# Spreading the reloads of the half-transformed rows over the slots of a fused Fourier mixer and feed-forward kernel on Trainium2

## The chip, the cores and the metric

The kernel runs on one core of one Trainium2 chip. The time is device microseconds of one execution. The engines named below are TensorE (PE; PEld is its weight load), VectorE (DVE), ScalarE (ACT), GpSimd (POOL) and SyncE (SP). SP and POOL issue the DMAs, each in the order of its own queue.

## The reference

```
X  = rfft(x, axis=1)                       # x: 8 x 3008 x 256, float32
Yr = Xr @ w_r - Xi @ w_i + b_r             # Yi likewise, 256 x 256 weights
Y  = softshrink(Yr, 0.01) + 1j * softshrink(Yi, 0.01)
a  = irfft(Y, n=3008, axis=1)              # 8 x 3008 x 256 = 24064 tokens
h  = relu(a @ w_in)                        # 256 -> 2048
out = (s * h * h + b) @ w_out              # 2048 -> 256, float32
```

## The kernel before, in words

All transforms are matmuls with tables of cosines and sines. The Fourier transform over 3008 points is split in two steps: batches 0 and 1 use 94 x 32, batches 2 to 7 use 64 x 47, whose tables are other ones. A batch passes through these stages, each a list of units that one call returns:

- `s1_units(b)` (L677): the first step of the transform, one matmul of 512 columns a unit (L702; L700 for batch 1). Its result `u` is evicted to SBUF (L248 on ACT or L252 on DVE, whichever the planner's running load favours) and stored to the DRAM tensor `ud` (L706). Batches 2 to 7 have 12 units and 6 stores of 256 KB. After the last unit four loads `us <- ud` (L712, 384 KB each) bring the rows back in another order of partitions: this is the exchange that the two-step transform needs. The pool of `us` has four buffers.
- `fwd_units(b)` (L719): the second step from `us` (L729) into `xt`. For batch 1 it is part of the mix (L763).
- `mix_units(b)` (L741): 12 mix units a batch. Sums (L793), the mixing by the weights (L806), bias and soft threshold on DVE (L811 to L818) into `ring`, then an exchange of rows between the halves of the partitions. For the first ten units this row swap is four DMAs of 32 KB on SP (`ring <- ring`, L826), for the last two four copies on DVE (L828). The inverse step reads the swapped rows two steps of the list later (L836), and its result `v` is stored to `vd` (L845). After the last unit two loads `vs <- vd` (L852, 768 KB each) exchange again.
- `s4_units(b)` (L876): the last inverse step from `vs` (L892) into `yt`.
- the feed-forward layer over 48 tiles of tokens: `first_mm` (L947) with Relu on ACT (L954), the square on DVE or ACT (L961, L958), `second_mms` (L1005), the scaling (L1015) and the stores of `out` on SP (L973, L980, L988).

One tile of the feed-forward layer takes 16 slots. A slot holds two matmuls of L947 and four of L1005, and a written plan says which units of the other stages go into which slot: `schedule(start, span, units)` spreads a list evenly over `span` slots. `mark[b]` is the slot at which batch b's tiles begin: 0, 96, 192, 272, 368, 464, 560, 656. So while the tiles of batch b-2 run, batch b goes through its first step and batch b-1 through its mix.

The plan gives the order in which the work is recorded. The tile framework then sets the order on each engine and the waits: POOL and SP start a DMA when their queue reaches it and its waits are met, not at a slot. Every DMA on SP takes the next of eight completion semaphores, and waits for the DMA eight places before it on SP to land.

The two tables of the second kind of transform, `F_v` (576 KB, into the buffer of `F_t`, L386) and the one in `T_t` (768 KB, L388), are loaded by POOL once batch 1 no longer reads the old ones: by `load_tables_2` (L384).

Of the kernel before, what the change touches and what calls it, by code (L numbers as in the profile page):

```python
# [9 lines left out]
F16 = mybir.dt.float16  # L10
# [4 lines left out]
P = 128  # L15
# [9 lines left out]
SLOTS = 48  # L25
GROUPS = 32
# [139 lines left out]
def kernel(  # L166
# [13 lines left out]
    nc = tc.nc  # L180
    B, S, D = x.shape
# [47 lines left out]
    uspool = ctx.enter_context(tc.tile_pool(name="usp", bufs=4))  # L229
# [13 lines left out]
    def evac(dst, src, cols, scale=None):  # L243
        ta, td = 0.17 + cols / 1200.0, 0.15 + cols / 960.0
        if load["act"] + ta <= load["dve"] + td:
            load["act"] += ta
            if scale is None:
                return None, nc.scalar.copy(out=dst, in_=src)  # L248
            return None, nc.scalar.mul(out=dst, in_=src, mul=scale)
        load["dve"] += td  # L250
        if scale is None:
            return nc.vector.tensor_copy(out=dst, in_=src), None  # L252
        return nc.vector.tensor_scalar_mul(out=dst, in0=src, scalar1=scale), None
# [8 lines left out]
    def any_bank():  # L262

        turn_of[0] += 1
        if "h" in pools:
            return (other_bank, one_bank)[turn_of[0] % 2]()
        return (mix_bank, one_bank, mix_bank, other_bank)[turn_of[0] % 4]()
# [4 lines left out]
    def one_bank():  # L272
        return fpool.tile([P, 512], F32, name="psf", tag="psf")
# [110 lines left out]
    def load_tables_2(i):  # L384
        if i == 0:
            nc.gpsimd.dma_start(out=F_v, in_=F_v_d)  # L386
        else:
            nc.gpsimd.dma_start(out=T_t, in_=T_v_d)  # L388
# [69 lines left out]
    us = {}  # L458
# [7 lines left out]
    def first_batch():  # L466
# [138 lines left out]
        def last_dft(ec, n):  # L605
# [17 lines left out]
            )  # L623

        more = s1_units(1, True)

        def some(n):
# [45 lines left out]


    UCH = XCH // 2

    def s1_units(b, more_banks=False):  # L677

        old = b == 1
        rows, n = (96, N2) if old else (P, XH)  # L680
        ud = dpool.tile([rows, n, D], F16, name="ud", tag="ud")
        hold = {}
        if old:
            xts[b] = bigpool.tile([P, 2 * DC * CLASSES * L1], F16, name="xt", tag="xt")

        def unit(i):
            c, j = divmod(2 * i, XCH)
            k, ju = divmod(2 * i, UCH)
            if ju == 0:
                if old and k % 2:  # L690
                    w = UCH * D
                    hold["u"] = xts[b][:, k // 2 * w : k // 2 * w + w].rearrange(
                        "p (j d) -> p j d", d=D
                    )
                else:
                    hold["u"] = upool.tile([P, UCH, D], F16, name="u", tag="u")
            ps = any_bank() if more_banks else one_bank()
            rhs = x16[(b, c)][:, j * D : (j + 2) * D]
            if old:
                nc.tensor.matmul(ps[0:96, :], A_t[0:N1, :], rhs[0:N1], start=True, stop=True)  # L700
            else:
                nc.tensor.matmul(ps, A_2, rhs, start=True, stop=True)  # L702
            u = hold["u"]
            evac(u[0:rows, ju : ju + 2, :], ps[0:rows].rearrange("p (j d) -> p j d", j=2), 512)
            if ju == UCH - 2:
                nc.sync.dma_start(out=ud[:, k * UCH : (k + 1) * UCH, :], in_=u[0:rows])  # L706
            if i == n // 2 - 1:
                p, g = (P, 6) if old else (2 * SLOTS, GROUPS // 4)
                uv = ud.rearrange("k n d -> (k n) d").rearrange("(q p) d -> p q d", p=p)
                for q in range(4):  # L710
                    t = uspool.tile([P, g, D], F16, name="us", tag="us")
                    nc.sync.dma_start(out=t[0:p], in_=uv[:, g * q : g * q + g, :])  # L712
                    us[(b, q)] = t

        return [lambda i=i: unit(i) for i in range(n // 2)]

    xts = {}

    def fwd_units(b):  # L719

        cuts = [(lo, 5) for lo in range(0, 20, 5)] + [(lo, 4) for lo in range(20, GROUPS, 4)]

        def unit(lo, w, dc):
            if b not in xts:
                xts[b] = bigpool.tile([P, 2, DC, CLASSES * L1], F16, name="xt", tag="xt")
            ps = one_bank()
            for j in range(w):
                q, g = divmod(lo + j, GROUPS // 4)
                nc.tensor.matmul(  # L729
                    ps[:, j * 96 : (j + 1) * 96],  # L730
                    us[(b, q)][0:96, g, dc * P : (dc + 1) * P], F_v[:, lo + j, :],
                    start=True, stop=True,
                )
            evac(
                xts[b][:, :, dc].rearrange("p r (x j) -> p r x j", j=GROUPS)[..., lo : lo + w],
                ps[:, 0 : w * 96].rearrange("p (j r x) -> p r x j", r=2, x=SLOTS), w * 96,
            )

        return [lambda c=c, dc=dc: unit(*c, dc) for c in cuts for dc in range(DC)]
# [136 lines left out]
    def s4_units(b):  # L876

        groups = []
        for lo in range(0, N2, 5):
            for ec in range(DC):  # L880
                groups.append((lo, min(5, N2 - lo), ec))

        def unit(g):
            n2, w, ec = groups[g]
            if g == 0:
                shape = [P, DC, N2, 96] if b == 1 else [P, DC, SLOTS * L1]
                yts[b] = ypool.tile(shape, F16, name="yt", tag="yt")
            yt = yts[b]
            ps = one_bank()
            for j in range(w):  # L890
                h, k = divmod(n2 + j, HW)
                nc.tensor.matmul(  # L892
                    ps[:, j * 96 : (j + 1) * 96],
                    vs[(b, h)][:, k, ec * P : (ec + 1) * P], C_t if b == 1 else C_2,
                    start=True, stop=True,
                )
            if b == 1:
                evac(
                    yt[:, ec, n2 : n2 + w, :],
                    ps[:, 0 : w * 96].rearrange("p (j n) -> p j n", n=96), w * 96,  # L900
                )
                return
            evac(
                yt[:, ec].rearrange("p (n h m) -> p h n m", h=2, m=N2)[..., n2 : n2 + w],
                ps[:, 0 : w * 96].rearrange("p (m h n) -> p h n m", h=2, n=SLOTS), w * 96,
            )
            if g == len(groups) - 1:
                pr, half = divmod(b, 2)
                if half == 0:
                    tails[pr] = tpool.tile([P, DC, 2, TAIL], F16, name="tail", tag="tail")  # L910
                nc.gpsimd.tensor_copy(out=tails[pr][:, :, half], in_=yt[:, :, N - TAIL : N])

        return [lambda g=g: unit(g) for g in range(len(groups))]
# [112 lines left out]
    plan = {}  # L1026

    def schedule(start, span, units):
        for i, u in enumerate(units):
            plan.setdefault(start + (i * span) // len(units), []).append(u)  # L1030
# [19 lines left out]
    plan.setdefault(18, []).append(load_x_2)  # L1050
    schedule(24, 42, mix_units(1))
    for i in range(2):
        plan.setdefault(66 + 6 * i, []).append(lambda i=i: load_tables_2(i))
    schedule(mark[1] - 11, 16, s4_units(1))
    for b in range(2, B):
        s0, s1, s2 = mark[b - 2], mark[b - 1], mark[b]
        if b == 2:
            schedule(s0 + 36, 22, s1_units(b))
            schedule(s1 - 16, 18, fwd_units(b))
        else:  # L1060
            schedule(s0 + 2, s1 - s0 - 48, s1_units(b))
            schedule(s1 - 28, 14, fwd_units(b))
        schedule(s1 + 3, s2 - s1 - 31, mix_units(b))
        schedule(s2 - 14, 12, s4_units(b))
        if b + 1 < B:
            plan.setdefault(s1 - 26, []).append(lambda b=b: emit_load_x(b + 1))
# [43 lines left out]
```

## Time and profile before

| | us |
|---|---|
| three runs | 852.38, 855.0, 859.67 (median 855.0) |
| the profiled execution, its time | 853.03 |
| the profiled execution, its span | 851.2 |
| PE busy in the span | 834.9 (98%) |
| DVE, ACT, POOL busy in the span | 691.8 (81%), 645.8 (76%), 53.9 (6%) |
| mean of bytes moved | 115 GB/s |
| us <- ud, L712 | 28 DMAs of 384 KB |
| ring <- ring, L826 | 280 DMAs of 32 KB |

The profile is of one execution. A row of the waits gives the waiting engine and line, what it waited for, the time in all, how often, and the longest. A row of the timeline gives start, duration, engine, line and operation, output and input; x4 says that four such instructions were merged, and what stands in brackets is the idle time before it and what ended it. SPq rows are the issuing of DMAs, not their moving. The windows give, for a stretch of the span, the busy time of PE, PEld, DVE, ACT and POOL, then the granted clock of PE (1.00 is full speed), the DMA share and GB/s.

### The profile page before, as it was taken

The page shows a single profiled execution, that of the slowest core. Times are in us where ns is not written, and L with a number is a line of the kernel's source. Part 1 is how long each engine was busy: PE and PEld are TensorE (multiplying, and loading weights), DVE is VectorE, ACT ScalarE, POOL GpSimd, SP SyncE. Part 2 cuts the span into 40 slices and gives each one's busy share as a digit, 9 for nine tenths or more (in the row PEclk, how much of TensorE's full clock was granted, in tenths as well). Part 3 has the DMA queues.
Part 4 walks back from the last instruction along what each step waited for, and adds up shares of the span by engine and source line. Part 5 has one row for each costly group of instructions (what it writes and reads, how often), then busy time and mean ns, then how long its engine had stood idle before and what let it go on. Part 6 is the DMA issues. An engine that isn't in the chain of part 4 may idle for free.

```text
span 851.2 us, 17222 instructions
## 1 busy us (share of the span) xinstructions
PE 834.9 (98%) x6726; PEld 599.1 (70%) x6726; DVE 691.8 (81%) x999; ACT 645.8 (76%) x849; POOL 53.9 (6%) x87
## 2 busy tenths in 40 slices
PE   8999999999999989999999999999999999999998
PEld 7857766777777657667776677766677776766766
DVE  5999976888889868888888887888888888776675
ACT  5988867778777867787787878788776877766663
POOL 4540100000000000000000000000000000000000
PEclk9999999999999999999999999999999999999999
DMA  8965785156723673145731548123650222401111
GB/s 198 186 165 136 187 199 162 44 129 156 179 74 84 157 198 107 57 118 135 199 89 52 134 141 197 36 75 118 159 137 29 58 89 90 112 32 38 38 44 51
DMA packets 110505, 97.70 MB, mean 115 GB/s; under 512 B 11212, under 2 KB 99280, under 8 KB 109080
## 3 DMA queue, kind: packets, MB, share of 16 engines
q1 hardware_dynamic: 103480, 80.61, 33.4%
q0 software_dynamic: 6944, 16.00, 11.3%
q8 instruction: 53, 0.87, 0.4%
q14 instruction: 28, 0.23, 0.1%
HBM read 55.34 MB, written 46.66 MB: 120 GB/s over the span
## 4 chain that ended last, share of the span: by engine, by line
PE 88%; DMA 3%; ACT 3%; DVE 3%; issue 2%; POOL 0%; SPq 0%; DVEq 0%; ACTq 0%; POOLq 0%
PE psa L1005 36%; PE psh L947 36%; PE psf L806 4%; PE psf L892 2%; PE psf L836 2%; PE psf L793 2%; PE psf L729 2%; PE psf L702 2%; ACT rt L954 1%; DMA x<-in_x_dram 1%; DMA ring<-ring 1%; PE psm L528 1%; DMA vd<-v 1%; DMA vs<-vd 1%; DVE gt L961 1%
## 5 line engine op out<-in xcount | busy, mean ns | idle before, releaser
L954 ACT ACTIVATE rt<-psh 128x1024 f32<-128x1024 f32 (+2 forms) x384 | 386.9, 1008 | 129.0 <-PE psh L947 128.3
L961 DVE TENSOR_TENSOR gt<-rt 128x1024 f16<-128x1024 f32 (+2 forms) x315 | 377.3, 1200 | 104.3 <-ACT rt L954 102.7
L1005 PE MATMUL psa<-w_out_t,gt 128*128 128x256 f16 (+1 forms) x3024 | 455.6, 273 | 0.1
L1005 PEld LDWEIGHTS <-gt 128*128 128x128 f16 (+1 forms) x3024 | 302.2, 101 | 187.0 <-issue 2.3
L947 PE MATMUL psh<-yt,w_in 128*128 128x512 f16 (+1 forms) x1344 | 398.9, 380 | 0.2 <-ACT rt L954 0.2
L947 PEld LDWEIGHTS <-w_in 128*128 128x128 f16 x1536 | 141.5, 98 | 25.2 <-issue 1.9
L1015 DVE SCALAR_TENSOR_TENSOR ost<-psa,s_bc,bias_bc 128x512 f32<-128x512 f32 (+2 forms) x97 | 71.0, 732 | 15.7 <-PE psa L1005 14.9
L958 ACT ACTIVATE gt<-rt 128x1024 f16<-128x1024 f32 (+2 forms) x69 | 72.6, 1053 | 1.5
L248 ACT CAST v<-psf 128x512 f16<-128x512 f32 x79 | 45.8, 580 | 23.4 <-PE psf L836 23.4
L811 DVE TENSOR_TENSOR ring<-psf,s 128x512 f16<-128x512 f32 x84 | 57.5, 685 | 2.5 <-PE psf L806 1.0
L947 PE MATMUL psh<-tail,w_in 128*128 128x512 f16 (+1 forms) x192 | 52.2, 353 | 0.0
L806 PE MATMUL psf<-W_g,xt 128*128 128x256 f16 x336 | 50.4, 273 | 0.1
L248 ACT CAST xt<-psf 128x480 f16<-128x480 f32 (+3 forms) x74 | 43.0, 581 | 9.3 <-PE psf L729 8.2
L248 ACT CAST yt<-psf 128x480 f16<-128x480 f32 (+2 forms) x68 | 41.0, 622 | 11.4 <-PE psf L892 10.8
L248 ACT CAST u<-psf 128x512 f16<-128x512 f32 (+1 forms) x68 | 40.0, 588 | 1.0 <-PE psf L702 0.9
L816 DVE TENSOR_TENSOR ring<-ring,low 128x512 f16<-128x512 f16 x84 | 35.6, 423 | 2.3
L836 PE MATMUL psf<-ring,T_t 128*128 128x256 f16 x168 | 33.0, 275 | 4.3 <-DMA ring<-ring 4.1
L818 DVE TENSOR_TENSOR ring<-ring 128x512 f16<-128x512 f16 x84 | 35.5, 423 | 2.1
L817 DVE TENSOR_TENSOR ring<-ring,high 128x512 f16<-128x512 f16 x84 | 35.5, 422 | 2.0
L806 PEld LDWEIGHTS <-xt 128*128 128x128 f16 x336 | 32.9, 98 | 4.1 <-issue 0.2
L302 POOL DMA_DIRECT2D x<-in_x_dram x36 | 18.7, 528 | 237.4 <-PE psf L702 237.4
L892 PEld LDWEIGHTS <-vs 96*128 96x128 f16 x448 | 28.8, 97 | 6.7 <-issue 2.4
(114 smaller groups left out, 516.6 us busy)
## 6 DMA issues: line engine op xcount, KB each, us to landing
out_dram<-ost SPq DMA_DIRECT2D x170, 128.0 KB
us<-ud SPq DMA_DIRECT2D x28, 384.0 KB
vd<-v SPq DMA_DIRECT2D x42, 256.0 KB
vs<-vd SPq DMA_DIRECT2D x14, 768.0 KB
x<-in_x_dram POOLq DMA_DIRECT2D x36, 256.0 KB, 5.3
ud<-u SPq DMA_DIRECT2D x36, 256.0 KB
ring<-ring SPq DMA_DIRECT2D x280, 32.0 KB
out_dram<-ost SPq DMA_DIRECT2D x16, 120.0 KB
```

The lines of the kernel that those rows point to most:

```text
L248: return None, nc.scalar.copy(out=dst, in_=src)
L806: nc.tensor.matmul(ps[:, r, :], x_of(i, 1 - r)[:, dc], W_g[:, dc, r], start=(dc == 0), stop=(dc == DC - 1),)
L811: nc.vector.tensor_tensor(out=t, in0=ps, in1=hold[i // 2][:, i % 2].unsqueeze(1).to_broadcast([P, 2, D]), op=ALU.add,)
L816: nc.vector.tensor_tensor(out=m, in0=t, in1=low, op=ALU.max)
L836: nc.tensor.matmul(ps[:, j, :], T_t[:, 2 * i + j, :], z[:, j, :], start=True, stop=True)
L892: nc.tensor.matmul(ps[:, j * 96 : (j + 1) * 96], vs[(b, h)][:, k, ec * P : (ec + 1) * P], C_t if b == 1 else C_2, start=True, stop=True,)
L947: nc.tensor.matmul(o, w_in_t[dc][:, mc * P : (mc + 1) * P], r, start=(dc == 0), stop=(dc == DC - 1),)
L954: nc.scalar.activation(out=rt[:, :, 0:w], in_=ps[:, :, 0:w], func=AF.Relu)
L958: nc.scalar.activation(out=gt[:, :, 0:w], in_=rt[:, :, 0:w], func=AF.Square)
L961: nc.vector.tensor_tensor(out=gt[:, :, 0:w], in0=rt[:, :, 0:w], in1=rt[:, :, 0:w], op=ALU.mult)
L1005: nc.tensor.matmul(ps[0:size, h, :], gts[(ti, mc // 2)][:, mc % 2, sub * size : (sub + 1) * size], w_out_t[:, mc, :], start=(mc == 0), sto ...
L1015: nc.vector.scalar_tensor_tensor(out=ost[0:size, 0:k], in0=ps[0:size, 0:k], scalar=s_bc[0:size], in1=bias_bc[0:size].unsqueeze(1).to_broad ...
```

## The change

The four loads of `us` of batches 2 to 7 leave the last unit of the first step and become units of their own in the plan: for batch 2 at slots 69, 71, 73 and 75, for batches 3 to 7 at slots s1-48, -44, -40 and -36 (s1 is `mark[b-1]`). The first step of batches 3 to 7 is compressed by four slots, the forward units of batch 2 begin three slots later and end one later, and the two table loads are recorded at slots 54 and 80 instead of 66 and 72. Batch 1 keeps its four loads at the last unit. Some lines of the file move by one to seven.

```
@@ s1_units @@
-            if i == n // 2 - 1:
-                p, g = (P, 6) if old else (2 * SLOTS, GROUPS // 4)
-                uv = ud.rearrange("k n d -> (k n) d").rearrange("(q p) d -> p q d", p=p)
+            if i == n // 2 - 1 and old:
                 for q in range(4):
-                    t = uspool.tile([P, g, D], F16, name="us", tag="us")
-                    nc.sync.dma_start(out=t[0:p], in_=uv[:, g * q : g * q + g, :])
-                    us[(b, q)] = t
+                    load_us(q)
+
+        def load_us(q):
+            p, g = (P, 6) if old else (2 * SLOTS, GROUPS // 4)
+            uv = ud.rearrange("k n d -> (k n) d").rearrange("(q p) d -> p q d", p=p)
+            t = uspool.tile([P, g, D], F16, name="us", tag="us")
+            nc.sync.dma_start(out=t[0:p], in_=uv[:, g * q : g * q + g, :])
+            us[(b, q)] = t
+
+        us_loads[b] = [lambda q=q: load_us(q) for q in range(4)]
@@ the plan @@
     for i in range(2):
-        plan.setdefault(66 + 6 * i, []).append(lambda i=i: load_tables_2(i))
+        plan.setdefault(54 + 26 * i, []).append(lambda i=i: load_tables_2(i))
...
             schedule(s0 + 36, 22, s1_units(b))
-            schedule(s1 - 16, 18, fwd_units(b))
+            schedule(s0 + 69, 8, us_loads[b])
+            schedule(s1 - 13, 16, fwd_units(b))
         else:
-            schedule(s0 + 2, s1 - s0 - 48, s1_units(b))
+            schedule(s0 + 2, s1 - s0 - 52, s1_units(b))
+            schedule(s1 - 48, 16, us_loads[b])
             schedule(s1 - 28, 14, fwd_units(b))
```

In the built program the queue of POOL holds the same instructions in the same order, and both table loads wait for the same matmuls as before: F_v for the last L763 of batch 1, T_t for the last L836 of batch 1. The first instructions that stand elsewhere are, on PE, the forward units of batch 2, and on SP what follows the first `us` load of batch 2. The SP queue around the two places that matter below:

```
batch 2, before: last ud, us us us us, vd vd, out out, vd, vs vs
batch 2, after:  last ud, us, vd, us us, vd, out out, vd, us, vs vs
batch 4, before: swap 7, ud, last ud, swap 8, us us us us, out out, swap 9, vd
batch 4, after:  swap 7, last ud, us us, swap 8, out out, swap 9, vd, us us
```

For batches 3, 5, 6 and 7 the loads stand behind the last row swap both before and after. (The swaps named here are those of the preceding batch, whose mix runs beside the first step: for batch 4, of batch 3.)

More of the change, by code (lines that the diff above doesn't have):

```diff
@@ L675 @@
     UCH = XCH // 2
+    us_loads = {}
     def s1_units(b, more_banks=False):
```

## The prediction

> **What bounds the kernel now.** I read the page's busy times first, then who PE waits for, then the granted clock round those waits, then SP's queue just before them.
>
> ```profile
> PE 834.9 (98%) x6726; PEld 599.1 (70%) x6726; DVE 691.8 (81%) x999; ACT 645.8 (76%) x849; POOL 53.9 (6%) x87
> ```
>
> PE is busy for all but 16 us of the span. Some 8 of these lie in the start (4.7 us idle in the first 45 us) and the end (3.4 us in the last 51). The change adds or removes no matmul, so all that it can win is PE's waiting in between. The waits of PE from 60 us on:
>
> ```profile
> PE psf L836 <- DMA ring<-ring: 4.1, 3, 2.4
> PE psf L892 <- DMA vs<-vd: 1.8, 1, 1.8
> PE psf L892 <- ACT yt L248: 0.8, 3, 0.3
> PE psf L892 <- DVE yt L252: 0.6, 2, 0.3
> ```
>
> The reader should see that DMA makes PE wait at four moments only, 5.9 us in all. In PE's timeline they stand at 112.25 (0.44) and 114.57 (1.17), call them place A, at 139.02 (place B) and at 311.74 (place C):
>
> ```profile
> 139.02 0.39 PE L892 MATMUL psf<-C_t,vs 96*128 96x96 f16 x5 [1.82 <-DMA vs<-vd]
> ...
> 307.17 0.38 PE L836 MATMUL psf<-ring,T_t 128*128 128x256 f16 x2
> ...
> 311.74 0.62 PE L836 MATMUL psf<-ring,T_t 128*128 128x256 f16 x2 [2.44 <-DMA ring<-ring]
> ```
>
> A wait can cost more than its idle time. The windows just behind the three places (the column after the busy times is the granted clock):
>
> ```profile
> 115.10:118.70 3.60, 3.60 (x15) 2.32 (x14) 1.82 (x2) 2.19 (x3) 0.00 (x0) 0.53 0.38 126
> 139.10:143.00 3.90, 3.90 (x48) 3.03 (x49) 2.28 (x3) 3.10 (x6) 0.00 (x0) 1.00 0.50 144
> 313.30:316.70 3.40, 3.40 (x15) 1.82 (x13) 1.87 (x2) 1.66 (x3) 0.00 (x0) 0.51 0.63 197
> ```
>
> Behind A the clock is 0.53 for 3.6 us, which loses 3.6 x 0.47 = 1.7 us; behind C it is 0.51 for 3.4 us, again 1.7; behind B it stays 1.00. So A costs 1.6 + 1.7 = 3.3 us, B 1.8, C 2.4 + 1.7 = 4.1: together 9.2 us, 1.1% of the time. That is the ceiling.
>
> Why C waits is in SP's queue:
>
> ```profile
> 293.03 2.45 SPq L826 DMA_DIRECT2D ring<-ring  x4
> 295.58 1.01 SPq L706 DMA_DIRECT2D ud<-u  x2
> 296.69 3.06 SPq L826 DMA_DIRECT2D ring<-ring  x4
> 300.76 2.50 SPq L712 DMA_DIRECT2D us<-ud  x4
> 303.37 2.15 SPq L980 DMA_DIRECT2D out_dram<-ost  x2
> 305.62 3.49 SPq L826 DMA_DIRECT2D ring<-ring  x4
> ```
>
> The rows of swap 9 were ready at 298.2 (end of L818 on DVE), but SP stood until 300.76 for the last `u` store to land, issued four loads and two stores, and came to swap 9 at 305.62. By the trace's completion semaphores the loads landed at 304.69, 306.51, 309.34 and 310.92, one after another, and the swap right behind them at 311.5 to 312.0. PE wanted it at 309.3.
>
> **The change part by part.** *Place C, batch 4.* The new queue is: swap 7, last `u` store, two loads, swap 8, two stores, swap 9, a `v` store, two loads. The last `u` unit is four slots earlier on PE, but SP runs about 4 us behind DVE here (swap 7 was ready at 288.9 and issued at 293.03), and the store stands behind swap 7 in both orders. So I take the store at 296, its landing at 300.5 (before: 296.20 to 300.69, 4.5 us) and the two loads issued by 301.5, landing like the first two now at 304.6 and 306.4. What is now queued behind their wait is swap 8, which was ahead of it. It is issued until 304 and lands some 0.5 us behind the second load (swap 9 took 311.53 to 312.03 for its four), at 306.6 to 307.1; its reader starts at 307.17. Swap 9 is issued from 305 to 308, 8 places behind the first load, so that no third load stands before it, and lands 2 us later (swaps outside bursts: 1.9 us at 290), the last part at 309.5 to 310; its readers start at 309.3. Left of the wait: 0.3 us, too short to have moved the clock in any row above (A's 0.44 alone did not). Gain 2.1 + 1.7 = 3.8. Bounds: at best the whole 4.1; at worst the `u` store lands as late as the slowest of its kind (issued 205.28, landed 212.85: 7.6 us, 3.1 later than taken), swap 8 is 3.1 us late, and the place costs 3.4 + 1.7 = 5.1, a loss of 1.0.
>
> [...] The rows differ: 2.44 us at C and 1.17 us at A were followed by half rate, while 1.82 us at B was not. [...]
>
> *Place B, batch 2.* The two `vs` loads wait for the last `vd` store, which stood behind all four `us` loads: issued 126.39, landed 133.09. The queue was draining without a pause, with the fourth load landing 3.6 us behind the third (125.03, 128.64; T_t's load by POOL runs beside it from 119.4), 1.9 us where nothing does (216.87, 218.64, 220.41). One load now goes behind that store, which so lands 1.8 us sooner, at 131.3. The load then fills the pause between the store's last bytes and SP's next issue (the DMA share in 130 to 135 us is 0.37), so `vs` comes at about 137.1 instead of 138.97. PE comes to its reader earlier too: two of four forward units that stood before it now come later, 2 x 0.22 us, at 136.65. The wait falls from 1.8 to 0.5: gain 1.3. Bounds: 1.8, or a loss: the fourth load delays `vs` by its full 3.6 us and the clock falls, 3.6 + 1.7 = 5.3.
>
> *Place A* lies ahead of the first moved instruction on every engine, behind F_v's load (issued 100.00, landed 106.5) and an `x` load (105.91). Moving the table loads in the plan moves nothing: POOL's order and the waits for the last L763 and the last L836 are as before. I cost it at 0; if A went too, that would be 3.3 more.
>
> *What becomes tighter.* Forward units: the fourth load of batch 2 comes about 10 us after the first, at some 133 us, and its first reader is the unit of slot 94, near 144; in batches 3 to 7 the readers come over 10 us after the loads. Covered, at nothing; without that cover each late load would cost up to the 1.9 us between two landings. Between the last forward unit and the first sum of batch 2 two slots are left (1.7 us with their other work 2.1) instead of three; an eviction (0.5), two additions (0.4 each) and one square (1.2) in front of them make 2.5: up to 0.4 us. First-step units now often follow a mix unit at once, so that both evictions of a pair fall together; the two `psf` banks are then needed again after two slots. Batch 1's mix has such pairs already, and PE lost 0.1 us there in each of three stretches of 5 us. Five stages make 0.2 to 0.5. Together I take 0.6; bounds 0 and 3, the upper by 0.3 us (the longest wait for an eviction, L892) at two pairs in each of five stages.
>
> *Sum:* 853.0 (the profiled execution) - 3.8 - 1.3 + 0.6 = 848.5. It stood 2.0 us below the median of its runs, 855.0. The same offset gives **850.5**; as the slower of those runs should hold more such waits than the profile, I say 850.
>
> **The rivals.** *All waits go, and those of the slow runs too.* The run of 859.67 has 6.6 us that the profile does not show; if they are swaps late behind the loads as at C, the new order takes them as well, and the median comes to the profile's own level or, with A gone, to 848.5 - 3.3 = 845.2. For it: four loads in a row stand before each batch's `v` stores. Against: A's instructions do not move, and in batches 3, 5, 6 and 7 the loads already stood behind all swaps. 845.
>
> *C only changes its name.* SP stands for the last `u` store in front of swaps 8 and 9 instead of 9 alone. If the store lands 2 us later than taken, swap 8 is 2 us late, the clock falls and 3.7 of C's 4.1 are back; with B as predicted the execution takes 853.0 - 0.4 - 1.3 + 0.6 = 851.9, the median 854. For it: SP's 4 us of lag. Against: the loads in front are half as many.
>
> *Slower: evictions in pairs.* Where a mix unit (L806) and a first-step unit (L702) follow each other at once, the next but one needs the first one's bank after two slots, 1.74 us. If DVE, 81% busy and with squares of 1.2 us in front, takes longer than that, PE idles; from about 1.2 us on (A's second wait) the clock falls too. That is 1.2 + 1.7 = 2.9 us in each of the five stages of batches 3 to 7, 14.5 us: 848.5 + 14.5 = 863, the median 865. Against: batch 1's pairs cost next to nothing. One stage alone would cost only what B and half of C bring.
>
> **How the numbers follow.** Forecast 0.50, all waits go 0.24, C only changes its name 0.16, slower 0.10. The range runs from 844.0 (the first rival less a microsecond of scatter) to 857.0 (C's name changed, and the upper 3 us of the tighter places); above lies the slower rival's 0.10, below and beside it another 0.10. A change of 1%, 8.5 us, is about what this kernel's runs, 852.4 to 859.7, can tell from none. Faster than 846.5 are most of the first rival (0.20) and a tenth of all from the forecast: 0.30. Slower than 863.5: 0.10. Within: 0.60.
>
> **What would show it.** Right at C: PE's wait for `ring` near 311 under 1 us and the clock 1.00 behind it, with two `us` loads ahead of swap 8. Right at B: PE's wait for `vs` near 139 under 1 us and the last `vd` store landed by 132. A: waits of 0.4 and 1.2 us with the clock near 0.5 behind, as now. Wrong: PE waits longer for `ring` in batch 4, now at swap 8; or a new wait of PE for DVE or ACT in the mix of batches 2 to 6; or a wait of L729 for `us`.

## The result, and the profile after

| | before | after |
|---|---|---|
| median, 22 runs each, us | 855.44 (849.87 to 860.53) | 851.17 (848.47 to 853.61) |
| the profiled execution: its time, its span | 853.03, 851.2 | 851.1, 849.3 |

The ratio is 0.9949, with a 95% interval of 0.9932 to 0.9966: 4.3 us less at the median. In the file after, most lines that matter stand five lower (L836 is L841, L892 is L897, L826 is L831, L845 is L850); L702 is L703, L706 is L707, L712 is L716.

The busy times on the page, and PE's waits from 60 us on (engine, line, what it waited for: us in all, times, longest):

```profile
PE 832.3 (98%) x6726; PEld 598.4 (70%) x6726; DVE 691.5 (81%) x996; ACT 646.7 (76%) x852; POOL 55.1 (6%) x87
```

```profile
PE psf L841 <- DMA ring<-ring: 2.6, 3, 1.9
PE psf L897 <- DMA vs<-vd: 2.1, 1, 2.1
PE psf L897 <- ACT yt L248: 1.0, 4, 0.3
PE psf L897 <- DVE yt L252: 0.8, 3, 0.3
PE psf L703 <- DVE ring L816: 0.4, 1, 0.4
PE psf L734 <- ACT xt L248: 0.3, 1, 0.3
PE psf L841 <- DVE ring L816: 0.3, 1, 0.3
```

Waiting for DMA has gone from 5.9 to 4.7 us, and small waits for DVE and ACT have come: 1.4 us before, 2.8 now. PE's timeline shows the three places of the prediction, A (first two rows), B and C:

```profile
114.06 0.28 PE L841 MATMUL psf<-ring,T_t 128*128 128x256 f16 x1 [1.93 <-DMA ring<-ring]
115.69 0.65 PE L841 MATMUL psf<-ring,T_t 128*128 128x256 f16 x2 [0.47 <-DMA ring<-ring]
...
138.26 0.39 PE L897 MATMUL psf<-C_t,vs 96*128 96x96 f16 x5 [2.09 <-DMA vs<-vd]
...
308.09 0.54 PE L841 MATMUL psf<-ring,T_t 128*128 128x256 f16 x2 [0.22 <-DMA ring<-ring]
...
310.20 0.38 PE L841 MATMUL psf<-ring,T_t 128*128 128x256 f16 x2
```

At C 0.22 us are left of 2.44, now at the reader of swap 8; the reader of swap 9 (310.20) does not wait. A and B look no better than before: 2.4 us against 1.6, and 2.09 against 1.82. Behind C the granted clock (the column after the five busy times) is now full:

```profile
311.30:314.70 3.40, 3.40 (x26) 2.34 (x24) 2.67 (x4) 2.81 (x4) 0.00 (x0) 1.00 1.09 248
```

SP's queue at C (rows of issuing):

```profile
295.96 2.39 SPq L831 DMA_DIRECT2D ring<-ring  x4
298.44 0.54 SPq L707 DMA_DIRECT2D ud<-u  x1
300.71 0.92 SPq L716 DMA_DIRECT2D us<-ud  x2
301.74 2.40 SPq L831 DMA_DIRECT2D ring<-ring  x4
304.19 1.05 SPq L985 DMA_DIRECT2D out_dram<-ost  x2
305.35 3.22 SPq L831 DMA_DIRECT2D ring<-ring  x4
308.67 0.53 SPq L850 DMA_DIRECT2D vd<-v  x1
309.25 1.15 SPq L716 DMA_DIRECT2D us<-ud  x2
```

The order is the predicted one: two loads, swap 8, two stores, swap 9 (issued from 305.35), a `v` store, two loads.

To see where 1.9 us of span went, I matched PE's instructions of the two executions and read off how much earlier or later the first feed-forward matmul of certain slots starts. The same is done for every kernel of the experiments; minus is a gain, in us. A unit of 0.2 us that stands before this matmul in one kernel and behind it in another moves a figure by as much.

| | slots 60 to 68 (A) | 80 to 104 (B) | 104 to 232 | 232 to 288 (C) | 288 to 767 | one profile, in all |
|---|---|---|---|---|---|---|
| after | -0.92 | +0.98 | +0.36 | -3.80 | +1.06 | -2.2 |
| e1, batch 4 alone | -1.93 | +2.06 | -0.22 | -4.48 | -0.08 | -4.2 |
| e2, all but batch 4 | +0.31 | -1.22 | +0.42 | +1.94 | +0.98 | +3.3 |
| e3, tables' slots alone | -1.68 | +2.09 | 0 | +1.48 | +0.02 | +2.3 |
| e4, first step not compressed | +2.62 | -0.77 | +0.09 | -4.52 | +0.01 | -2.5 |
| e5, forward units not moved | -1.09 | -0.95 | -0.14 | -4.25 | +0.96 | -4.7 |
| e10, loads spread alone | -1.75 | -0.49 | 0 | -4.52 | +0.01 | -5.8 |
| e6, T_t later | -1.00 | -0.67 | +0.36 | -4.34 | +1.04 | -4.0 |
| e7, F_v and an x load later | -3.93 | +5.47 | +0.35 | -4.01 | +1.06 | -0.9 |
| e8, e10 with all three later | -3.93 | -1.72 | 0 | -4.52 | +0.01 | -9.5 |

(Left out: what precedes slot 60, +0.3 to +1.1, and slots 68 to 80, 0 or -0.2.) In A, all but e7 and e8 run the same instructions as before, so its column there, from -1.9 to +2.6, shows how far single executions of the same work differ at that place. At C the eight kernels with the new order lie between -3.80 and -4.52; the three executions with the old order lie at 0 (before), +1.48 (e3) and +1.94 (e2), so the execution before that was profiled was the mildest of them.

### The profile page after: what moved, and what is told of

Read it like the earlier page. It is cut to its first block, busy times and chain, and to the rows that moved or that the text cites. A ratio compares the mean times of both kernels' runs of the same rounds, so it can differ in the third digit from the quotient of the medians.

```text
span 849.3 us, 17221 instructions
## 1 busy us (share of the span) xinstructions
PE 832.3 (98%) x6726; PEld 598.4 (70%) x6726; DVE 691.5 (81%) x996; ACT 646.7 (76%) x852; POOL 55.1 (6%) x87
## 4 chain that ended last, share of the span: by engine, by line
PE 83%; DVE 6%; DMA 4%; ACT 4%; issue 3%; SPq 0%; POOL 0%; DVEq 0%; ACTq 0%; POOLq 0%
PE psa L1010 34%; PE psh L952 33%; PE psf L811 4%; DVE gt L966 2%; PE psf L798 2%; PE psf L841 2%; PE psf L897 2%; PE psf L734 2%; ACT rt L959 2%; DMA ring<-ring 2%; PE psf L703 2%; PE psm L528 1%; ACT yt L248 1%; DVE ring L816 1%; DMA vd<-v 1%
## 5 line engine op out<-in xcount | busy, mean ns | idle before, releaser
L963 ACT ACTIVATE gt<-rt 128x1024 f16<-128x1024 f32 (+2 forms) x66 | 69.2, 1049 | 1.8
L248 ACT CAST v<-psf 128x512 f16<-128x512 f32 x82 | 47.5, 579 | 22.7 <-PE psf L841 22.7
L841 PE MATMUL psf<-ring,T_t 128*128 128x256 f16 x168 | 32.6, 273 | 3.0 <-DMA ring<-ring 2.6
L897 PEld LDWEIGHTS <-vs 96*128 96x128 f16 x448 | 28.8, 97 | 7.9 <-issue 3.5
L916 POOL COPY tail<-yt 128x896 f16<-128x896 f16 x6 | 6.7, 1114 | 420.1 <-ACT yt L248 420.1
```

The source lines that it names most:

```text
L841: nc.tensor.matmul(ps[:, j, :], T_t[:, 2 * i + j, :], z[:, j, :], start=True, stop=True)
L897: nc.tensor.matmul(ps[:, j * 96 : (j + 1) * 96], vs[(b, h)][:, k, ec * P : (ec + 1) * P], C_t if b == 1 else C_2, start=True, stop=True,)
L963: nc.scalar.activation(out=gt[:, :, 0:w], in_=rt[:, :, 0:w], func=AF.Square)
```

## The experiments

Ratios are to the kernel before, timed together with the kernels of each group (its median 855.5 for e1, e2, e4 and e5, 854.66 for e6, e7, e8 and e10, 855.27 for e3). The kernel after was timed apart from all of them, so that it is compared with them by ratios.

**e1: the new order for batch 4 alone.** The kernel before, with

```
-            if i == n // 2 - 1:
+            if i == n // 2 - 1 and b != 4:
...
-            schedule(s0 + 2, s1 - s0 - 48, s1_units(b))
+            schedule(s0 + 2, s1 - s0 - (52 if b == 4 else 48), s1_units(b))
+            if b == 4:
+                schedule(s1 - 48, 16, us_loads[b])
```

> The kernel before with one part of the change: only batch 4's four loads are units of their own (and its first step four slots shorter); SP then has one load ahead of swap 9 and three behind it. Theory 1 (the gain is place C, where four loads stood ahead of swap 9): PE's wait for ring near 311 us falls from 2.4 us to under 0.5 and the clock stays 1.00 behind it, 4.1 us less, about 851, ratio 0.995. Rival (the gain comes from spreading the loads of all batches): at most a sixth of it, about 854.7, ratio 0.999.

Measured: 849.69 us, ratio 0.9924 (0.9895 to 0.9952). PE's waits for DMA from 60 us on:

```profile
PE psf L897 <- DMA vs<-vd: 2.6, 1, 2.6
PE psf L841 <- DMA ring<-ring: 1.5, 1, 1.5
```

The wait for `ring` is A's; C has none, and 4.48 us of the stretch are gone. One place, one batch, is worth all that the whole change brings. At B, where the instructions are those of before, this execution lost 2.06 us more than before's did. SP's queue at C is not that of after: swap 8 stands ahead of the loads, and one load ahead of swap 9.

```profile
301.78 0.40 SPq L716 DMA_DIRECT2D us<-ud  x1
302.27 2.49 SPq L831 DMA_DIRECT2D ring<-ring  x4
306.44 1.79 SPq L716 DMA_DIRECT2D us<-ud  x3
```

So swap 9 is issued from 302.27 instead of 305.62, and its last part landed at 307.69 instead of 312.03. In after it is issued about when it was before (305.35), but with two loads ahead of it and not four, and its last part landed at 309.88: 0.3 us before its reader came.

**e2: everything but batch 4.** The kernel after, with

```
-            if i == n // 2 - 1 and old:
+            if i == n // 2 - 1 and (old or b == 4):
...
-            schedule(s0 + 2, s1 - s0 - 52, s1_units(b))
-            schedule(s1 - 48, 16, us_loads[b])
+            schedule(s0 + 2, s1 - s0 - (48 if b == 4 else 52), s1_units(b))
+            if b != 4:
+                schedule(s1 - 48, 16, us_loads[b])
```

> The changed kernel with batch 4 put back: its four loads stand again in one row directly ahead of swap 9; all other batches as changed. Theory 1: the wait of 2 to 3 us for ring near 311 us and the half clock behind it are back, and what the other parts cost (2.5 us between slot 80 and the end by the matched matmuls) makes it 855 to 858, ratio 1.000 to 1.003. Rival (all batches): five sixths of the gain stay, about 852, ratio 0.996.

Measured: 856.4 us, ratio 1.0012 (0.9992 to 1.0033): no gain is left. SP's queue, PE's wait and the windows at C (busy times of PE, PEld, DVE, ACT, POOL, granted clock, DMA share, GB/s):

```profile
303.04 4.06 SPq L716 DMA_DIRECT2D us<-ud  x4
307.19 3.61 SPq L831 DMA_DIRECT2D ring<-ring  x4
```

```profile
313.84 0.74 PE L841 MATMUL psf<-ring,T_t 128*128 128x256 f16 x2 [4.14 <-DMA ring<-ring]
```

```profile
310.75:314.16 3.41, 0.28 (x1) 0.10 (x1) 0.56 (x1) 0.00 (x0) 0.00 (x0) 1.00 0.90 224
314.16:317.58 3.42, 3.40 (x13) 1.81 (x14) 1.75 (x2) 1.61 (x2) 0.00 (x0) 0.50 0.27 81
```

Four loads ahead of swap 9, a wait of 4.14 us and half rate behind it. With e1 this shows the cause of C from both sides: the burst of four loads in front of the swap.

**e4 and e5: the two edits around the loads.** e4 is the kernel after with the first step not compressed; e5 is the kernel after with the forward units of batch 2 where they were.

```
e4:
-            schedule(s0 + 2, s1 - s0 - 52, s1_units(b))
+            schedule(s0 + 2, s1 - s0 - 48, s1_units(b))
e5:
-            schedule(s1 - 13, 16, fwd_units(b))
+            schedule(s1 - 16, 18, fwd_units(b))
```

> The changed kernel with the first step of batches 3 to 7 spread over as many slots as before; the loads are still units of their own, in batch 4 one ahead of swap 9. Theory: the compression is what lost about 1.5 us in small waits of PE for evictions after C (the matched matmuls drift from -3.9 to -2.2 us between slot 264 and the end), so this one is 1 to 2 us faster than the changed kernel, 849.5 to 850, ratio 0.993 to 0.994. Rival (the compression is needed so that the last u store is down before the loads): C's wait comes back at least half, 853, ratio 0.997.

> The changed kernel with the forward units of batch 2 at their old slots 80 to 96. Theory: the 1.0 us that the changed kernel loses between slots 80 and 100 is the crowding of forward and last-step units there, so this is 0.5 to 1 us faster, 850.2 to 850.7, ratio 0.994. Rival (that 1.0 us is the longer wait for vs alone, PE coming earlier to it): no difference in the sum, 851, ratio 0.995, and the wait for vs shorter by 0.4 us, the two more forward units that stand before it.

Measured: e4 848.03, ratio 0.9913 (0.9886 to 0.9941); e5 849.2, ratio 0.9924 (0.9896 to 0.9952). In the table, about 1 us (0.96 to 1.06) of slots 288 to 767 stands in every kernel whose first step is compressed in all of batches 3 to 7, or all but batch 4 (after, e2, e5, e6, e7), and in no other. The moved forward units add 0.46 or 0.47 us between slots 88 and 104 in every kernel that has them, and 0.0 in e1, e3, e5, e8 and e10. The 0.35 to 0.42 of slots 104 to 232 stand only where both are (after, e2, e6, e7). By the ratios alone neither edit is told from after: the intervals overlap.

**e10: the loads spread, nothing else.** e4's edit and e5's together. The loads remain units and the tables' slots are those of after.

> The change without the compression of the first step and without the move of batch 2's forward units: only the loads as units of their own. Theory: it keeps the gain at C and loses nothing in small waits, about 848, ratio 0.991. Rival (the two other edits are needed): 851, ratio 0.995.

Measured: 846.91 us, ratio 0.9897 (0.9873 to 0.9921). The two edits around the loads cost the change as much as it brought in all: 0.9949 (0.9932 to 0.9966) with them, 0.9897 without. A part of that is C: in e1, e4, e8 and e10 swap 8 goes ahead of the loads and one load ahead of swap 9, and they read -4.48 to -4.52 there; in after, e5, e6 and e7 two loads go ahead of swap 8, and they read -3.80 to -4.34.

**e3: the tables' slots alone.** The kernel before, with

```
-        plan.setdefault(66 + 6 * i, []).append(lambda i=i: load_tables_2(i))
+        plan.setdefault(54 + 26 * i, []).append(lambda i=i: load_tables_2(i))
```

> The kernel before with the two table loads recorded at slots 54 and 80 and nothing else. Its instructions stand on every engine in the order of the kernel before. Theory (slots do not bind POOL): no difference, ratio 0.998 to 1.002, place C's wait of 2 to 4 us with half clock behind it as before, and the waits at A and B differing from the kernel before by up to 2 us, as they do between executions whose instructions up to there are the same. Rival (the table slots are part of the gain): F_v or T_t issued at other times than 100 and 119 us and a ratio under 0.998.

Measured: 854.85 us, ratio 0.9985 (0.9955 to 1.0014): no difference. F_v's load is issued at 100.4 and T_t's at 118.1, about as before (100.0 and 119.4). What releases POOL, and not the slot, sets them.

**e6: T_t's load held back behind `vs`.** The kernel after, with a copy of one element from batch 1's `yt` into T_t ahead of T_t's load, so that it waits until the last inverse step has begun to be evicted.

```
+            nc.gpsimd.tensor_copy(out=T_t[0:1, 0, 0:1], in_=yts[1][0:1, 0, 0, 0:1])
...
-        plan.setdefault(54 + 26 * i, []).append(lambda i=i: load_tables_2(i))
+        plan.setdefault(54 + 36 * i, []).append(lambda i=i: load_tables_2(i))
```

> The changed kernel with the load into T_t held back until the last inverse step of batch 1 has written its first rows (about 139 us instead of 119; its reader comes at 168). Theory (T_t's 768 KB run beside the v stores and hold vs back at place B): from the last L836 of batch 1 to the landing of vs it takes 16 us instead of 17 to 20, PE's wait at B is 0 to 0.5 us in place of 0 to 2.1, the time falls by about 1, ratio 0.994. Rival (SP's own queue of loads and stores is the limit there): the lag stays at 17 to 20 us and the ratio at 0.995.

Measured: 849.97 us, ratio 0.9933 (0.991 to 0.9955). PE at A and B:

```profile
116.08 0.66 PE L842 MATMUL psf<-ring,T_t 128*128 128x256 f16 x2 [2.49 <-DMA ring<-ring]
...
137.02 0.39 PE L898 MATMUL psf<-C_t,vs 96*128 96x96 f16 x5 [0.45 <-DMA vs<-vd]
```

From the last inverse matmul of batch 1 to the landing of `vs` took 20.2, 20.9 and 20.9 us with the burst (before, e1, e3), 20.0, 17.2, 18.9, 19.2 and 19.6 with the new order (after, e2, e4, e5, e10), and 18.4 here, where 16 was expected. That lies among those that do not hold T_t back, and the ratio too is not told from that of after: no gain from T_t alone is shown.

**e7: F_v's load and batch 4's `x` load held back.** The kernel after, with the same device: F_v behind the last row of `ring` that batch 1 writes in A, the `x` load behind batch 1's `yt`; F_v's load is recorded at slot 66.

```
+            nc.gpsimd.tensor_copy(out=F_t[0:1, 0, 0:1], in_=ring[0][0:1, 11, 0, 0:1])
...
+            if second is not None:
+                nc.gpsimd.tensor_copy(out=t[L1 : L1 + 1, 0:1], in_=second)
...
-        plan.setdefault(54 + 26 * i, []).append(lambda i=i: load_tables_2(i))
+        plan.setdefault((66, 54)[i] + 26 * i, []).append(lambda i=i: load_tables_2(i))
...
-            plan.setdefault(s1 - 26, []).append(lambda b=b: emit_load_x(b + 1))
+            plan.setdefault(s1 - 26, []).append(lambda b=b: emit_load_x(b + 1, *([yts[1][r : r + 1, 0, 0, 0:1] for r in (0, L1)] if b == 3 else [])))
```

> The changed kernel with F_v's load held back until DVE has written the rows of unit 11 (113 us instead of 100), and batch 4's first x load until after 139 us. Theory (these 576 KB and 512 KB stand beside swaps 8 and 9 at place A): the swaps land 2 to 3 us after their issue instead of 4 to 8, PE's waits for ring at 112 to 117 us go, and with them 1.6 to 3.3 us; F_v then runs beside the v stores and may make vs up to 2.7 us later. Net 0 to 3 us faster, ratio 0.992 to 0.995. Rival (the swaps are late because of what SP itself has in its queue): the waits at A stay at 1.5 us or more.

Measured: 851.88 us, ratio 0.9958 (0.9932 to 0.9984). A has no wait at all: the last part of swap 9, issued at 109.33, landed 2.5 us later (3.1 in e8); in the kernels that hold neither load back it took 4.1 to 6.5. So these two loads together are the cause of A; what each of them costs was not tried. But F_v now runs beside T_t and the `us` loads, and B pays for it:

```profile
113.71 0.53 POOL L389 DMA_DIRECT2D F_t<-dft_fwd  x1 [0.32 <-POOL F_t L388]
...
115.86 0.56 POOL L391 DMA_DIRECT2D T_t<-dft_inv  x1 [1.62 <-PE psf L844]
```

```profile
138.14 0.58 PE L900 MATMUL psf<-C_t,vs 96*128 96x96 f16 x5 [4.91 <-DMA vs<-vd]
```

`vs` came 22.8 us behind the last inverse matmul; with the wait of 4.91 us came half rate from 135.85 to 142.67 us (granted clock 0.50). A's gain of 3.0 us against after (-3.93 for -0.92) was given back at B and more (+5.47 for +0.98).

**e8: e10 with all three loads held back.** e10's two edits, e7's copies and e6's.

> The loads as units of their own, the first step and batch 2's forward units in their old slots, and T_t, F_v and batch 4's first x load held back as in the two kernels above. Theory: places A, B and C all go, 9 us off the kernel before without the small waits of the compression: 845 to 846.5, ratio 0.988 to 0.990, faster than every kernel so far. Rival (what is held back only collides later, with us, vd and vs): no better than the same kernel without the holding back, 848, ratio 0.991.

Measured: 844.0 us (843.5 to 845.1), ratio 0.9864 (0.9837 to 0.9891): 10.7 us faster than before. After's own ratio, 0.9949, lies far outside the interval. All of PE's waits from 60 us on that the view names, and POOL's two table loads:

```profile
PE psf L901 <- ACT yt L248: 0.8, 3, 0.3
PE psf L901 <- DVE yt L252: 0.6, 2, 0.3
```

```profile
113.98 0.53 POOL L389 DMA_DIRECT2D F_t<-dft_fwd  x1 [0.32 <-POOL F_t L388]
...
135.73 0.56 POOL L392 DMA_DIRECT2D T_t<-dft_inv  x1
```

The view names no wait for DMA any more, and `vs` lands at 134.0, just as PE comes to it. What A was made of is to be seen in the windows from 105 us (after first, then e8; the last two columns are the DMA share and GB/s):

```profile
105.00:112.00 7.00, 7.00 (x53) 5.33 (x51) 6.56 (x16) 5.90 (x9) 1.04 (x2) 1.00 0.87 201
```

```profile
105.00:112.00 7.00, 7.00 (x53) 5.46 (x52) 6.56 (x16) 5.90 (x9) 0.00 (x0) 1.00 0.48 143
```

Until A the swaps of 32 KB ran beside F_v and an `x` load that nobody needed yet; with the two held back the DMA share in this stretch is 0.48 instead of 0.87.

## Why the prediction was right, and where not

The median was forecast at 850 and measured at 851.17, 4.3 us less than before where 4.5 was forecast. The mechanism, place C, was right; that the figure came so close is in part luck. The sum gave 848.5 for an execution like the profiled one, and this took 851.1. The 1.5 us that lay between the sum and the forecast, as an offset of the median from the profile, measured 0.1 in after. By the table, the profile missed the sum at two terms: B, where 0.5 us were lost beside the forward units instead of 1.3 gained, and what becomes tighter, 1.9 instead of 0.6; A gave 0.9 back by its scatter. Step by step:

- **Place C: right, by a chain with one lucky link.** 3.8 was predicted, 3.80 came (4.0 to 4.5 in e1, e4 to e8 and e10). The landings, by completion semaphores, are near those worked out: the two loads 304.8 and 306.4 (304.6, 306.4 predicted), swap 8 306.6 to 308.3 (306.6 to 307.1), swap 9 308.9 to 309.9 (309.5 to 310). The `u` store landed at 300.7 (300.5), but it was issued at 298.44 and not at 296, and took 2.2 us and not 4.5: two errors that cancel. The tail of swap 8 was a miss too. PE came to its reader at 307.87; at 307.17, as taken, it would have waited for 0.9 us and not 0.22.
- **The clock at C: the row was right.** The wait's removal brought more than the wait itself in all these kernels, 3.8 to 4.5 against 2.44, and the granted clock behind C is full (1.00) in all of them.
- **Place B: near it as a mean of few executions, wrong in the profile of after.** PE's wait there was 1.82, 2.56 and 2.56 us with the burst (before, e1, e3), mean 2.3, with half rate behind two of the three (0.50 from 137.85 us in e1 and from 138.06 in e3). It was 2.09, 0, 0.34, 0.86 and 1.32 with the new order (after, e2, e4, e5, e10), mean 0.9, and never half rate (granted clock 1.00). The means differ by 1.4 in wait alone; 1.3 was predicted. The step that failed in the execution shown is the landing of the last `vd` store, 132.4 instead of 131.3:

```profile
118.85 0.34 SPq L716 DMA_DIRECT2D us<-ud  x1
...
126.15 1.06 SPq L850 DMA_DIRECT2D vd<-v  x1
...
132.46 0.81 SPq L857 DMA_DIRECT2D vs<-vd  x2
```

The first `us` load was issued at 118.85, not at 117.05 as before, because the last `u` store of batch 2 had landed at 118.84 and not at 117.03; swap 9 at A, ahead of it on SP, landed 1.1 us later too (116.0 against 114.9). So A's scatter seems to reach B. PE also came to its reader at 136.17, 0.5 us before the 136.65 that was taken (the prediction's own figures, 139.02 - 1.82 - 0.44, give 136.76).

- **Place A: nothing changed, as costed,** since no instruction in it moved. The sign that was named, 0.4 and 1.2 us and half rate behind, was too exact: with the same instructions the waits were 1.5 to 3.3 us together, with half rate (0.50) behind those of before, e2 and e4 and full rate (1.00) behind those of after, e1, e3, e5, e6 and e10.
- **What becomes tighter: the mis-sized term.** 0.6 was taken. By e4, e5 and e10 it measured 0.47 (forward units) + 0.36 (slots 104 to 232) + 1.06 (the stretch from slot 288, by the compression) = 1.9 us in the profile. By the ratios of after and e10 it is 4.4 us (0.0052 of 855), with C's part in it; that lies outside the bounds 0 and 3, and what makes up the rest is open. The forecast of the median still held, it seems, because C and B brought more than their terms: the old order's C cost 1.5 and 1.9 us more in e3 and e2 than in the profile before, and the half rate behind B in e1 and e3 was not in that profile either.
- **The rivals.** "C only changes its name" fell: swap 8 did come behind the store's wait, but PE waited 0.22 us for it and not 2. "Slower: evictions in pairs" was far too dear: the new waits for evictions and sums (L703, L734, L841) are 0.3 to 0.4 us each, never 1.2, moved no clock (1.00 from 20 to 840 us in after), and the compression cost 1.06 us in the profile, 3 by the ratios of after and e4, where 14.5 were put. Its condition, half rate from waits of 1.2 us on, does not hold either: 1.17 us was A's second wait, and after waits of 2.09 us (after) and 2.41 us (e5) the clock stayed full. "All waits go" is not what this change does, for the reason given: A's instructions stay. e8, another kernel that holds back A's and B's transfers too, reaches 844.0, about the level that rival named.
- **Tables' slots: right,** by e3.

Open: why single executions differ at A by up to 4.5 us with the same instructions; what of B keeps `vs` 18.4 us behind when T_t is held back; why the two edits cost 4.4 us by the ratios and 1.9 in the profile; and the new order for batch 2 alone, which was not tried.

## What to carry to other kernels

In this kernel a swap of 32 KB on the critical path landed behind the loads of 384 KB that were ahead of it in its queue (C: the last load at 310.92 us, the swap at 311.5 to 312.0), and took 4.1 to 6.5 us instead of 2.5 and 3.1 where large transfers of another queue were under way (A). So issue a batch of prefetches one by one behind the small transfers, and hold back by a data dependence what nobody needs yet: the slot in the written order didn't hold POOL's queue here (e3: issued at 100.4 and 118.1 us, against 100.0 and 119.4 before). Make room for such transfers without moving compute: here the edits that made room cost half of the gain. And when a hidden transfer is moved, look what it meets in its new place: F_v and an `x` load cost 3 us at A, and F_v cost 4.5 at B in e7, where T_t and the `us` loads ran beside it; in e8, with T_t held back too and without the two edits, this cost is gone.

## What the runs showed of the hardware that was not expected

From 63 to 321 us of the eleven executions, the half rate (granted clock 0.50) came in stretches of 3.41 us (115.25 to 118.66 and 313.22 to 316.64 before, 137.85 to 141.26 in e1) or twice that (115.54 to 122.37 in e4), whose edges lie elsewhere in each execution. In these rows it does not go with how long one wait was. Each pair of rows gives 3.41 us with a wait, or a part of it, in them and the 3.41 us that follow: the kernel before at C, e5 at A, and e6 at A:

```profile
309.81:313.22 3.41, 1.43 (x10) 0.94 (x11) 0.55 (x1) 0.83 (x2) 0.00 (x0) 1.00 0.71 216
313.22:316.64 3.42, 3.42 (x15) 1.83 (x13) 1.90 (x2) 1.68 (x3) 0.00 (x0) 0.50 0.65 202
```

```profile
111.99:115.40 3.41, 1.53 (x13) 1.05 (x10) 3.32 (x7) 1.50 (x2) 0.00 (x0) 1.00 0.85 221
115.40:118.81 3.41, 2.79 (x20) 1.95 (x21) 1.37 (x3) 2.01 (x4) 0.00 (x0) 1.00 0.29 93
```

```profile
111.48:114.90 3.42, 2.11 (x16) 1.43 (x13) 3.30 (x8) 1.56 (x3) 0.00 (x0) 1.00 0.74 218
114.90:118.31 3.41, 2.14 (x15) 1.45 (x15) 1.28 (x2) 1.54 (x3) 0.00 (x0) 1.00 0.45 139
```

Of the wait of 2.44 us before (309.30 to 311.74) 1.9 us fell into the first row shown, PE was busy for 1.43 us of it, and half rate followed. Of the wait of 2.41 us in e5 1.9 us fell into one row too, PE was busy for 1.53 us, and full rate followed. The wait of 2.49 us in e6 (113.59 to 116.08) lies in both its rows, PE was busy for 2.1 us of either, and full rate followed. In the 3.41 us just ahead of the nine stretches of half rate PE was busy for 0.28 to 1.43 us eight times and for 1.71 once (before at A, with two waits in it); in the other rows of this length that were read at full rate it was busy for 1.53 and more. In e5 and e6 no change of the clock shows where such a row should begin, so this is a count of rows and not a rule. What followed these three waits of 2.4 to 2.5 us was 1.7 us more (half of 3.41) once and nothing twice; what decides between the two was not shown, and a single profile can't tell which is usual.
